# Key bits of the first head scaled on ScalarE, and one quarter of expert weights instead of two ahead of the first expert's tokens

## The chip, the cores and the metric

The kernel runs on one NeuronCore of one Trainium2 chip. Its engines work side by side, each through its own instructions in program order: PE (TensorE, matmuls; its weight loads are a row of their own, PEld), DVE (VectorE), ACT (ScalarE), POOL (GpSimd) and SP (SyncE, which here only issues DMAs). POOL also issues the DMAs that gather or scatter rows by an index. The metric is the device time of one execution in microseconds (us).

## The reference

Bucketed attention feeds a mixture of experts. Attention: a query and a key may meet only where the signs of six random projections agree.

```python
q_bits = (np.einsum('bhsd,dk->bhsk', q, proj) > 0)      # (4, 8, 768, 64) x (64, 6); k likewise
mask   = q_bucket[:, :, :, None] == k_bucket[:, :, None, :]
scores = np.where(mask, scale * np.matmul(q, k.transpose(0, 1, 3, 2)), -1e9)
attn   = softmax(scores); out = np.matmul(attn, v)
```

Mixture of experts on the 3072 rows of `out` (512 columns): tokens are assigned greedily, highest gate logit first, each of the 8 experts taking at most 384; then for each expert

```python
h = np.maximum(x[mask] @ w1[e], 0.0)     # w1: (8, 512, 1024)
out[mask] = h @ w2[e]                    # w2: (8, 1024, 512)
```

## The kernel before, in words

**Attention** takes the 32 heads in groups of four. Every float32 operand is split into a high and a low 16-bit half, so that products of halves replace one float32 product. The six sign bits of a query or key are six more rows of the stationary and moving operands `qa` and `ka`, scaled to plus or minus 4096 so that unequal buckets fall out of the softmax. `S_pass` (line 226) makes scores whose row maximum DVE takes (line 228), `m_rows` (line 241) writes that maximum back into `qa`, `ST` (lines 250 to 252) makes the scores again, transposed, with their exponential on ACT, and `AV` multiplies by the values.

**The opening** prepares the first group by hand, in the order written out in the string `OPS`: each word is a letter for a function and a number. `t0` (`top`) casts the first head's query and key, `b0` and `b1` (`tbits`) make the first head's query and key sign bits: PE projects (line 209), DVE compares and writes plus or minus 0.5 (line 210), and DVE multiplies by 8192 (line 211). `r0 r2 r1 r3` (`rest`, line 214) cast the halves for `qb` and `kb` on ACT, `c1 c0` (`cast`, line 123) those of heads 2 and 3, `l0 l1 l3 l2` (`rlo`, lines 216 and 217) and `u0 u1` (`sub`, line 126) subtract on POOL. `B0` and `D0` (`bits`, lines 134 to 140, and `bdma`, line 309) make the sign bits of the other three heads: PE projects, DVE compares into `bt` (line 139), DVE scales `bt` (line 140), and SP sends it off. The words `w2`, `w4`, `w5` are idle matmuls on `wrm` (line 72), whose result nobody reads.

**Routing** sorts tokens to experts in phases, one an expert; phase 0 decides who goes to expert 0, and so on. A phase is a chain of short steps that go between DVE (compare, line 496) and PE (count, lines 507 and 514). Phases 1 to 7 are run beside the previous expert's matmuls, at fixed steps of that work: phase 1 at the steps `E1`.

**The transition** (`start`) comes after phase 0 has found which rows of the weights and of the tokens expert 0 needs. `wload` has POOL gather weights (line 721): expert 0's first matrix in four quarters (128 x 1024 float32, 0.52 MB each), its second in two halves (1.05 MB each). `gather` has POOL fetch the 384 tokens in three pieces `xg` (line 713, 0.26 MB each). `wsplit` splits a quarter: ACT scales it into the high half `wh` (line 730) and the low half `wl` is made by DVE for the first two quarters (line 734), later by an ACT scaling (line 731) and a subtraction on POOL. `xsplit0` transposes a token piece on PE (line 766), ACT writes the high half `xh` (line 767) and DVE the low half `xl` (line 768); then come idle matmuls (`warm`, line 540), 7 after each piece, by `KW[6]`. `KW[5]` idle matmuls stand behind the last matmul of phase 0 (line 698), before the first piece.

**The experts** then run in steps of three matmuls of the first layer (line 780, 128x384 each, twelve to a block `f`, ACT's `hh` at line 782 after each block) or two of the second (line 792). The weights of expert 0's second matrix are split from step 2 on, ahead of the first `hh` in ACT's order.

The order on each engine is the order in which the Python code emits it (`manual_schedule`); waits are put in by the framework.

Of the kernel before, what the change touches and what calls it, by code (L numbers as in the profile page):

```python
# [14 lines left out]
ALU = mybir.AluOpType  # L15
# [27 lines left out]
def attention(tc, nc, ctx, qT, kT, vv, proj, wg, x_dram, L, jp, identf, B, late=None, after=None):  # L43
# [6 lines left out]
    V=nc.vector; A=nc.scalar; G_=nc.gpsimd; T=nc.tensor; SY=nc.sync  # L50
# [74 lines left out]
    def sub(G,w,p,eng=None):  # L125
        (eng or G_).tensor_tensor(TMP[G,'l'][w][:,p],LD[G][w][:,p],TMP[G,'h'][w][:,p],op=ALU.subtract)
# [78 lines left out]
    def tbits(w):  # L205
        dst=(QA,KA)[w][0][64:70,0,0:S]
        for hf in range(2):
            ps=psT.tile([128,512],F32,name="pst"); r=slice(hf*384,hf*384+384)
            T.matmul(ps[64:70,0:384],prt,(qd,kd)[w][0:64,0,r],start=True,stop=True,tile_position=(0,64))
            V.tensor_scalar(dst[:,r],ps[64:70,0:384],0.0,0.5,op0=ALU.is_gt,op1=ALU.subtract)  # L210
        V.tensor_scalar(dst,dst,8192.0,None,op0=ALU.mult)
    def rest(j,n):
        h=slice(64,128) if n<2 else slice(0,64); dst,src=((QB,qd),(KB,kd),(QB,qd))[n]
        A.copy(dst[0][h,j],src[h,j])
# [95 lines left out]
    def copies(a):  # L310
        for j in (0,2): SY.dma_start(a[1][64:128,j:j+2,0:S],a[0][64:128,2:4,0:S])
    OPS=dict(i=lambda j: init(j,A.copy),t=top,b=tbits,r=lambda n: rest(n//3,n%3),l=lambda n: rlo(n//2,n%2),
        c=lambda w: cast(0,w,1),u=lambda w: sub(0,w,1),s=lambda k: S_pass(k//6,k%6),B=lambda n: bits(0,[1]),D=lambda n: bdma(),
# [46 lines left out]
    for t in range(6*NH+LAG+6):  # L360
        h,s=divmod(t,6)
# [29 lines left out]
W2=[2,7,12,17]  # L391
XS=[56,56,57,57]
XD=[0,8,7,4]
KW=[1,0,4,0,2,19,7,1]
SC=16
XSC=8.0
WSC=64.0
class Moe:
# [143 lines left out]
    def phase(s,ph):  # L542
# [9 lines left out]
        if not last:  # L552
# [13 lines left out]
            for l,w in enumerate(WID):  # L566
# [3 lines left out]
                if l==0 or first:  # L570
# [3 lines left out]
                    if first:  # L574
                        if l==0: wp=s.wps(); s.warm(KW[7],wp)
                        s.warm(KW[0],wp)
                    for a,b in ((l+1,l+2),) if first else ((1,6),):
# [18 lines left out]
                T.matmul(n,s.us[l][0:J if first else 128],hit[0:J if first else 128],start=True,stop=True)  # L596
                if first: s.warm(KW[1],wp)
                elif l==0 and ph>1:
# [14 lines left out]
            T.matmul(pe[:,0:8],s.tiny,sat,start=False,stop=True)  # L613
            if first: s.warm(KW[2],wp)
            V.reduce_max(nn,pe[:,0:8],axis=AX.X)
# [24 lines left out]
        T.matmul(pp[:,0:2*NC],s.ones,cum,start=False,stop=True)  # L640
        if first: wp=s.psO.tile([128,512],F32,name="po"); s.warm(KW[3],wp)
        elif not last: s.fill()
# [32 lines left out]
        if first:  # L675
            pi=ps()
            for i,b in enumerate(blocks):
                members(*b)
                if not i: rr()
                collect(*b); s.warm(KW[4],wp)  # L680
        else:
# [76 lines left out]
    def xsplit0(s):  # L758

        xh,xl=s.W[0,'x']=(s.t([128,4,384],F16,"xh",bufs=1),s.t([128,4,384],F16,"xl",bufs=1))  # L760
        V=s.nc.vector; A=s.nc.scalar
        for c in range(3):
            px=(s.psX,s.psX,s.psA)[c].tile([128,512],F32,name=("px","px","psa")[c])
            r=slice(c*128,c*128+128); p4=px.rearrange("p (d q) -> p d q",d=4)
            for d in range(4):
                s.nc.tensor.transpose(p4[:,d],s.XG[0][:,c,d*128:d*128+128],s.identf)
            A.mul(xh[:,:,r],p4,XSC)  # L767
            V.scalar_tensor_tensor(xl[:,:,r],p4,XSC,xh[:,:,r],op0=ALU.mult,op1=ALU.subtract)
            s.warm(KW[6],s.wp)

    def layer1(s,ph,f,piece):
        T=s.nc.tensor
# [32 lines left out]
    def start(s):  # L805

        s.ps0=None; V=s.nc.vector
        s.wload(0,0,4,(0,1))
        next(s.ph0)
        s.gather(0)  # L810
        s.wload(0,0,4,(2,3))
        s.wsplit(0,0,0,V)
        next(s.ph0)
        s.ch=[s.phase(p) for p in range(8)]
        s.wsplit(0,0,1,V)
        s.wload(0,1,2)
        s.xsplit0()
        s.wsplit(0,0,2,by=14)
        s.wsplit(0,0,3,by=22)

# [86 lines left out]
```

## Time and profile before

| | us |
|---|---|
| three runs, median (lowest to highest) | 754.43 (754.01 to 759.91) |
| the profiled execution, its own time | 757.86 |
| its span, first to last instruction | 756.1 |
| PE busy in the span | 679.5 (90%) |
| DVE busy | 552.9 (73%) |
| ACT busy | 465.0 (61%) |
| POOL busy | 497.1 (66%) |

All durations below are from the one profiled execution, whose span is 756.1 us and which took 757.86 us in all, 3.43 us more than the median of the runs. "Idle before" in a row is the engine's own idle time ahead of that instruction, and the arrow names what ended it. The clock column of a table by stretch is TensorE's granted clock, 1.00 for 2.4 GHz and 0.50 for 1.2 GHz.

### The profile page before, as it was taken

To read this page: it belongs to the slowest core of one execution; us is meant where nothing else is said; L and a number is where in the kernel's file an instruction comes from. 1 tells how busy PE (TensorE), PEld (TensorE's weight loads), DVE (VectorE), ACT (ScalarE), POOL (GpSimd) and SP (SyncE) were. 2 spreads that over 40 slices of the span, in tenths; PEclk is the share of its full clock that TensorE was granted. 3 is DMA by queue.
4 is the path that set the end of the run, shared out by engine and by line. 5 is a ranking of instruction groups with operands and counts; after the bars stand their busy time and mean duration, and the time that the engine had idled before them with its cause. 6 is when DMAs were issued, how large, how long until landed. Compare 5 with 4: busy or idle time off the path is not lost. (4 is left out here: it accounts for less than half of the span.)

```text
span 756.1 us, 19028 instructions
## 1 busy us (share of the span) xinstructions
PE 679.5 (90%) x7789; PEld 438.1 (58%) x7789; DVE 552.9 (73%) x1178; ACT 465.0 (61%) x852; POOL 497.1 (66%) x436
## 2 busy tenths in 40 slices
PE   8898979999999999998988679999789899999995
PEld 2566656776767767666666454545445455555552
DVE  4979967888878888988985668676758878754120
ACT  6677666677776777665664063756547475756550
POOL 8587849697795977856664246474827382858671
PEclk9999999999999999999999589999999999999998
DMA  7638653625546255340001161616071717162611
GB/s 188 170 98 223 147 163 79 168 64 139 136 107 176 65 133 160 84 97 23 23 10 36 54 212 26 254 46 262 29 255 52 235 59 275 40 231 91 243 55 42
DMA packets 39951, 93.57 MB, mean 124 GB/s; under 512 B 4548, under 2 KB 30520, under 8 KB 37816
## 3 DMA queue, kind: packets, MB, share of 16 engines
q1 hardware_dynamic: 33048, 46.21, 23.5%
q0 software_dynamic: 6816, 46.15, 17.3%
q8 instruction: 61, 1.00, 0.6%
q14 instruction: 26, 0.21, 0.1%
HBM read 59.53 MB, written 12.58 MB: 95 GB/s over the span
## 5 line engine op out<-in xcount | busy, mean ns | idle before, releaser
L255 POOL TENSOR_TENSOR lo<-pt 128x768 f16<-128x768 f32 x143 | 233.8, 1646 | 78.3 <-ACT pt L252 64.8
L252 ACT ACTIVATE pt<-pst 128x384 f32<-128x384 f32 x384 | 182.9, 491 | 98.6 <-PE pst L251 85.6
L228 DVE TENSOR_REDUCE m<-pss 128x1 f16<-128x770 f32 x192 | 182.4, 955 | 38.2 <-PE pss L226 37.2
L250 PE MATMUL pst<-qa,ka 128*128 128x384 f16 x384 | 126.0, 328 | 6.7 <-DVE XT L294 3.6
L251 PE MATMUL pst<-qb,kb 128*128 128x384 f16 x384 | 125.9, 328 | 0.0
L267 PE MATMUL psv<-vh,lo 128*128 128x65 f16 x1152 | 121.6, 194 | 3.8 <-POOL lo L255 3.8
L265 PE MATMUL psv<-vh,pt 128*128 128x65 f16 x1152 | 121.8, 195 | 0.0
L266 PE MATMUL psv<-vl,pt 128*128 128x64 f16 x1152 | 121.8, 193 | 0.0
L265 PEld LDWEIGHTS <-pt 128*128 128x128 bf16 x1152 | 107.2, 98 | 13.0 <-issue 3.5
L266 PEld LDWEIGHTS <-pt 128*128 128x128 bf16 x1152 | 106.2, 99 | 9.8 <-issue 0.5
L267 PEld LDWEIGHTS <-lo 128*128 128x128 f16 x1152 | 106.2, 98 | 4.1 <-POOL lo L255 4.1
L226 PE MATMUL pss<-ka,qa 128*128 128x385 f16 x384 | 95.3, 330 | 14.1 <-DVE m L228 14.0
L730 ACT ACTIVATE wh<-wf 128x1024 f16<-128x1024 f32 x64 | 67.2, 1050 | 40.7 <-PE psa L698 21.1
L742 POOL TENSOR_TENSOR wl<-wf,wh 128x512 f16<-128x512 f32 x71 | 79.9, 1147 | 0.0
L780 PEld LDWEIGHTS <-wh 128*128 128x128 f16 x512 | 47.8, 97 | 39.3 <-issue 9.4
L731 ACT ACTIVATE wf<-wf 128x1024 f32<-128x1024 f32 x62 | 65.5, 1057 | 2.0
L783 DVE SCALAR_TENSOR_TENSOR hl<-px,hh 128x384 f16<-128x384 f32 x64 | 34.4, 551 | 41.2 <-ACT hh L782 40.8
L226 PEld LDWEIGHTS <-qa 128*128 128x128 f16 x384 | 37.5, 98 | 45.6 <-issue 23.2
L255 DVE TENSOR_TENSOR lo<-pt 128x768 f16<-128x768 f32 x49 | 61.0, 1246 | 1.5 <-ACT pt L252 1.0
L792 PEld LDWEIGHTS <-hh 128*128 128x128 f16 x384 | 36.5, 98 | 40.5 <-issue 2.5
L795 ACT ACTIVATE o<-po 128x512 f32<-128x512 f32 x24 | 14.2, 591 | 71.4 <-PE po L792 71.2
L780 PE MATMUL px<-xh,wh 128*128 128x384 f16 x256 | 53.2, 325 | 4.0 <-ACT xh L767 1.7
(253 smaller groups left out, 1328.1 us busy)
## 6 DMA issues: line engine op xcount, KB each, us to landing
vp<-in_vv_dram SPq DMA_DIRECT2D x8, 768.0 KB
x_dram<-X SPq DMA_DIRECT2D x16, 384.0 KB
qp<-in_qT_dram SPq DMA_DIRECT2D x7, 768.0 KB
kp<-in_kT_dram SPq DMA_DIRECT2D x7, 768.0 KB
qa<-qh SPq DMA_DIRECT2D x14, 192.0 KB
ka<-kh SPq DMA_DIRECT2D x14, 192.0 KB
qb<-qh SPq DMA_DIRECT2D x14, 192.0 KB
kb<-kh SPq DMA_DIRECT2D x14, 192.0 KB
```

The lines of the kernel that those rows point to most:

```text
L226: T.matmul(ps[:,hf,0:HK],QA[u][:,j,qc*128:qc*128+128],KA[u][:,j,hf*HK:hf*HK+HK],start=True,stop=True)
L228: V.tensor_reduce(M6[h][:,qc:qc+1],ps[:,:,0:HK],axis=AX.XY,op=ALU.max,negate=True)
L250: T.matmul(ps[:,0:384],KA[u][:,j,kr],QA[u][:,j,r],start=True,stop=False)
L251: T.matmul(ps[:,0:384],KB[u][:,j,kr],QB[u][:,j,r],start=False,stop=True)
L252: A.activation(PT[h,kc][0][:,r],ps[:,0:384],AF.Exp,scale=0.125)
L255: eng.tensor_tensor(l,p,p.bitcast(BF)[:,1::2],op=ALU.subtract)
L265: T.matmul(av[:,c,:],ph[:,r],VH[u][:,j,kc,:],start=(kc==0 and c==0),stop=False,skip_group_check=True)
L266: T.matmul(av[:,c,0:64],ph[:,r],VL[u][:,j,kc,:],start=False,stop=False,skip_group_check=True)
L267: T.matmul(av[:,c,:],l[:,r],VH[u][:,j,kc,:],start=False,stop=False,skip_group_check=True)
L730: s.nc.scalar.mul(h[:,r],f[:,r],WSC)
L742: for _ in range(n): s.nc.gpsimd.tensor_tensor(*s.pend.pop(0)[1],op=ALU.subtract)
L780: T.matmul(p[:,0:384],a[:,o:o+128],b[:,d],start=n==0,stop=n==11)
```

## The change

Four edits. In the opening, the scaling of the first head's key bits (`tbits(1)`, the word `b1`) goes from DVE to ACT; that of the query bits stays on DVE. In the transition, POOL gathers one quarter of the weights ahead of the tokens instead of two, and the split of the second quarter (`wsplit(0,0,1,V)`, one ACT and two DVE instructions) comes after the tokens' split instead of before it. The idle matmuls ahead of the first token piece go from 19 to 32. Those after the three pieces go from 7, 7, 7 to 6, 12, 7.

```diff
@@ tbits
-        V.tensor_scalar(dst,dst,8192.0,None,op0=ALU.mult)
+        if w: A.mul(dst,dst,8192.0)
+        else: V.tensor_scalar(dst,dst,8192.0,None,op0=ALU.mult)
@@
-KW=[1,0,4,0,2,19,7,1]
+KW=[1,0,4,0,2,32,(6,12,7),1]
@@ xsplit0
-            s.warm(KW[6],s.wp)
+            s.warm(KW[6][c],s.wp)
@@ start
-        s.wload(0,0,4,(0,1))
+        s.wload(0,0,4,(0,))
         next(s.ph0)
         s.gather(0)
-        s.wload(0,0,4,(2,3))
+        s.wload(0,0,4,(1,2,3))
         s.wsplit(0,0,0,V)
         next(s.ph0)
         s.ch=[s.phase(p) for p in range(8)]
-        s.wsplit(0,0,1,V)
         s.wload(0,1,2)
         s.xsplit0()
+        s.wsplit(0,0,1,V)
         s.wsplit(0,0,2,by=14)
         s.wsplit(0,0,3,by=22)
```

From line 211 on, a line of the kernel before has the next higher number in the changed one. **ACT in the opening**, from the first head's casts on (`qa`, `ka`: operands of the first head; `qb`, `kb`: their low parts' operands; `kh`, `qh`: halves of heads 2 and 3). Before:

```order
L204 CAST qa_167<-XT 64x768
L204 CAST ka_168<-XT 64x768
L214 CAST qb_169<-XT 64x768 x2
L214 CAST kb_170<-XT 64x768
L204 CAST qa_167<-XT 64x768
L204 CAST ka_168<-XT 64x768
L123 CAST kh<-kp 128x768
L123 CAST qh<-qp 128x768
```

Changed:

```order
L204 CAST qa_167<-XT 64x768
L204 CAST ka_168<-XT 64x768
L211 ACTIVATE ka_168<-ka_168 6x768
L215 CAST qb_169<-XT 64x768 x2
L215 CAST kb_170<-XT 64x768
L204 CAST qa_167<-XT 64x768
L204 CAST ka_168<-XT 64x768
L123 CAST kh<-kp 128x768
L123 CAST qh<-qp 128x768
```

The scaling stands third here, ahead of seven casts, and it reads what DVE wrote at line 210.

**ACT in the transition** (`wh_8728`: expert 0's first matrix, high half, a quarter to an instruction; the other `wh` and its `wf`: the second matrix). Before:

```order
L730 ACTIVATE wh_8728<-wf_8663 128x1024 x2
L767 ACTIVATE xh<-px 128x4x128 x2
L767 ACTIVATE xh<-psa 128x4x128
L730 ACTIVATE wh_8728<-wf_8663 128x1024
L731 ACTIVATE wf_8663<-wf_8663 128x1024
L730 ACTIVATE wh_8728<-wf_8663 128x1024
L731 ACTIVATE wf_8663<-wf_8663 128x1024
L730 ACTIVATE wh_8839<-wf_8764 128x1024
L731 ACTIVATE wf_8764<-wf_8764 128x1024
L782 ACTIVATE hh<-px 128x384
L582 ACTIVATE zE<-zD 128x24 x5
```

Changed:

```order
L731 ACTIVATE wh_8728<-wf_8663 128x1024
L768 ACTIVATE xh<-px 128x4x128 x2
L768 ACTIVATE xh<-psa 128x4x128
L731 ACTIVATE wh_8728<-wf_8663 128x1024 x2
L732 ACTIVATE wf_8663<-wf_8663 128x1024
L731 ACTIVATE wh_8728<-wf_8663 128x1024
L732 ACTIVATE wf_8663<-wf_8663 128x1024
L731 ACTIVATE wh_8856<-wf_8774 128x1024
L732 ACTIVATE wf_8774<-wf_8774 128x1024
L783 ACTIVATE hh<-px 128x384
L583 ACTIVATE zE<-zD 128x24 x5
```

The second quarter's instruction has moved from ahead of the three `xh` to behind them; all that follows is in the order it had.

**DVE in the transition** (`rem` to `nrem`: the end of phase 0; `zm`: the start of phase 1's decision). Before:

```order
L672 TENSOR_SCALAR nrem<-rem 128x8
L734 SCALAR_TENSOR_TENSOR wl_8729<-wf_8663,wh_8728 128x512 x2
L768 SCALAR_TENSOR_TENSOR xl<-px,xh 128x4x128 x2
L768 SCALAR_TENSOR_TENSOR xl<-psa,xh 128x4x128
L478 TENSOR_REDUCE zm<-Lm 128x24
```

Changed:

```order
L673 TENSOR_SCALAR nrem<-rem 128x8
L769 SCALAR_TENSOR_TENSOR xl<-px,xh 128x4x128 x2
L769 SCALAR_TENSOR_TENSOR xl<-psa,xh 128x4x128
L735 SCALAR_TENSOR_TENSOR wl_8729<-wf_8663,wh_8728 128x512 x2
L479 TENSOR_REDUCE zm<-Lm 128x24
```

The second quarter's low half now stands directly ahead of phase 1.

## Rows read from the trace of the kernel before

**Rows 1.** From the page: PE's busy share and its granted clock in 40 equal slices of the span, in tenths (9 is 90% or more).

```profile
PE   8898979999999999998988679999789899999995
...
PEclk9999999999999999999999589999999999999998
```

**Rows 2.** The timeline of the opening around the first head's bits, all engines: start, duration, engine, line, operation, and in brackets idle time before it and what ended it.

```profile
5.82 0.83 ACT L204 CAST ka<-XT 64x768 f16<-64x768 f32 x1
...
6.67 1.69 ACT L214 CAST qb<-XT 64x768 f16<-64x768 f32 x2
...
10.44 0.56 DVE L210 TENSOR_SCALAR ka<-pst 6x384 f16<-6x384 f32 x1 [0.20 <-PE pst L209]
...
11.03 0.45 DVE L211 TENSOR_SCALAR ka<-ka 6x768 f16<-6x768 f16 x1
...
12.87 0.15 PEld L226 LDWEIGHTS <-qa 128*128 128x128 f16 x1 [0.17 <-issue]
```

**Rows 3.** The same timeline, POOL's subtractions and a DVE instruction beside them.

```profile
7.92 1.64 POOL L217 TENSOR_TENSOR qb<-XT,qb 64x768 f16<-64x768 f32 x1
...
8.47 1.30 DVE L211 TENSOR_SCALAR qa<-qa 6x768 f16<-6x768 f16 x1
...
14.44 1.63 POOL L126 TENSOR_TENSOR kl<-kp,kh 128x768 f16<-128x768 f32 x1
```

**Rows 4.** Line 140, all eight of its instructions: durations in ns, shortest, median, longest.

```profile
L140 DVE TENSOR_SCALAR bt<-bt x8: 359/590/1654, 19.7 to 310.3; 128x768 f16<-128x768 f16 x8
```

**Rows 5.** The timeline behind the sign bits of the other heads, and the ends of the idle times of POOL and ACT there.

```profile
19.68 0.36 DVE L140 TENSOR_SCALAR bt<-bt 128x768 f16<-128x768 f16 x1
19.95 2.69 DVE L228 TENSOR_REDUCE m<-pss 128x1 f16<-128x770 f32 x3
...
20.96 0.49 PE L226 MATMUL pss<-ka,qa 128*128 128x385 f16 x2 [0.28 <-DVE m L228]
...
22.52 0.66 ACT L241 ACTIVATE qa<-pst,mbi,msc 32x384 f16<-32x384 f32 x1 [6.88 <-issue]
...
27.11 0.24 POOL L288 TENSOR_TENSOR wgs<-wgr,wgs 128x32 f16<-128x32 f32 x1 [9.32 <-issue]
```

**Rows 6.** POOL's timeline in the transition: weight quarters and halves (`wf`) and token pieces (`xg`). Other issues are left out.

```profile
428.93 1.14 POOL L721 DMA_INDIRECT wf<-in_w_dram,zwidx  x1 [20.55 <-DVE zmi L654]
...
432.71 0.95 POOL L713 DMA_INDIRECT xg<-x_dram,zidx  x1 [0.69 <-DVE zA L659]
...
436.65 0.98 POOL L721 DMA_INDIRECT wf<-in_w_dram,zwidx  x1 [0.30 <-issue]
```

**Rows 7.** PE's timeline from the end of phase 0 to the first layer.

```profile
433.17 2.19 PE L540 MATMUL po<-iot,mones 128*128 128x128 bf16 x19
436.81 1.12 PE L766 MATMUL px<-identf,xg 128*128 128x128 f32 x4 [1.45 <-DMA xg<-x_dram,zidx]
437.71 0.95 PE L540 MATMUL po<-iot,mones 128*128 128x128 bf16 x7
...
440.06 1.06 PE L766 MATMUL psa<-identf,xg 128*128 128x128 f32 x4
...
443.52 0.81 PE L780 MATMUL px<-xh,wh 128*128 128x384 f16 x4 [1.70 <-ACT xh L767]
```

**Rows 8.** ACT's timeline there and in the first steps of the first layer.

```profile
433.75 1.06 ACT L730 ACTIVATE wh<-wf 128x1024 f16<-128x1024 f32 x1 [21.08 <-PE psa L698]
435.87 1.06 ACT L730 ACTIVATE wh<-wf 128x1024 f16<-128x1024 f32 x1 [1.07 <-DMA wf<-in_w_dram,zwidx]
...
442.87 0.60 ACT L767 ACTIVATE xh<-psa 128x512 f16<-128x512 f32 x1 [2.71 <-remote]
...
447.44 1.04 ACT L730 ACTIVATE wh<-wf 128x1024 f16<-128x1024 f32 x1
...
449.85 0.66 ACT L582 ACTIVATE zE<-zD 128x24 bf16<-128x24 int32 x5
```

**Rows 9.** DVE and PE in the first steps of phase 1, from the timelines of both engines.

```profile
434.83 1.29 DVE L734 SCALAR_TENSOR_TENSOR wl<-wf,wh 128x512 f16<-128x512 f32 x2 [1.74 <-ACT wh L730]
...
444.11 0.34 DVE L478 TENSOR_REDUCE zm<-Lm 128x24 f32<-128x192 f32 x1
...
447.16 0.46 PE L507 MATMUL psa<-zOH,zcmp 128*128 128x8 bf16 x12 [0.55 <-DVE zcmp L496]
...
451.35 0.32 PE L514 MATMUL psa<-zOH,zcmp 128*128 128x32 bf16 x6 [0.84 <-DVE zcmp L496]
...
464.80 0.32 PE L514 MATMUL psa<-zOH,zcmp 128*128 128x32 bf16 x6 [0.83 <-DVE zcmp L496]
```

**Rows 10.** A table by stretch (start:end, length; busy us and instructions of PE, PEld, DVE, ACT, POOL; granted clock of PE; share of the DMA engines; GB/s). The first two stretches lie in attention, the others in the transition.

```profile
345.50:349.40 3.90, 1.96 (x39) 1.47 (x36) 3.83 (x6) 0.54 (x2) 2.40 (x2) 1.00 0.01 4
349.60:352.80 3.20, 3.00 (x15) 1.80 (x14) 2.22 (x5) 2.19 (x5) 1.47 (x1) 0.50 0.42 123
...
438.50:441.50 3.00, 3.00 (x23) 2.88 (x22) 1.38 (x2) 0.65 (x2) 2.39 (x3) 0.50 0.81 243
441.50:443.40 1.90, 0.32 (x4) 0.20 (x2) 0.00 (x0) 0.53 (x2) 0.20 (x1) 0.96 1.02 362
443.40:446.50 3.10, 2.98 (x18) 1.66 (x17) 2.97 (x12) 3.04 (x5) 0.00 (x0) 1.00 0.98 391
446.50:449.00 2.50, 1.53 (x30) 1.10 (x30) 2.06 (x9) 2.47 (x3) 0.00 (x0) 1.00 0.52 213
```

## The prediction

> **What bounds the kernel now.** Read the page first: PE is busy in nearly every slice, and its granted clock dips visibly in one place only, the 23rd and 24th slice, which are phase 0 and the transition [rows 1]. A microsecond lost ahead of PE's dense work is therefore lost at the end, and the change touches the two places where PE waits by design: the opening, up to 24 us, and the transition, from 428.9 to 451.4 us. I read each as a chain: who ends the wait of whom.
>
> In the opening, PE reaches the first scores at 12.87, through idle matmuls; the key bits are ready at 11.03 + 0.45 = 11.48 [rows 2], so line 211 binds nobody. The next thing that does is DVE: PE waits 0.28 at 20.96 for the first of three maxima, which follow line 140 on DVE without a gap [rows 5].
>
> In the transition PE ends its 19 idle matmuls and waits 1.45 for the first token piece, then works piece by piece at the low clock, and starts the first layer at 443.52 [rows 7]. What it gains there it can only keep if the next wait does not end later: PE stops again at 447.16 for phase 1's first compare and at 451.35 for the next one [rows 9]. These two waits end by other chains: DVE starts phase 1 at 444.11, and ACT makes `zE` at 449.85 at the end of a queue without a gap [rows 8, 9]. From 451.35 to the wait at 464.80 PE's timeline has no wait of note, so the time of the row at 451.35 is what the transition passes on to the end.
>
> **The scaling on ACT.** It removes 0.45 from DVE, which hides behind PE's idle matmuls: worth nothing. It adds one ACT instruction that cannot start before 10.44 + 0.56 = 11.00 and stands ahead of seven casts of which the first began at 6.67 [rows 2]. No row has this instruction on ACT; a cast of as many columns takes 0.83 (row at 5.82), DVE took 0.45, an ACT pass over 1024 columns 1.06 [rows 8]. I take 0.83 for the same column count, and 0.45 to 1.06 as bounds: done at 11.83, still 1.0 ahead of PE at 12.87. Without that cover it would cost its own excess over 0.45.
>
> The casts then run from 11.83 instead of 6.67, 5.16 later. ACT's own cover is the idle 6.88 before 22.52 [rows 5]: enough. POOL's first subtraction needs the first of the two casts: 11.83 + 1.69/2 = 12.7 instead of 7.92, so its unbroken row of six moves by 4.8. POOL's cover is the idle 9.32 before 27.11: enough too.
>
> But the move puts one of POOL's instructions beside line 140. The fifth, 14.44 to 16.07, goes to 19.2 to 20.9, and line 140 comes to its turn at 19.68. What that does is seen on DVE's instructions of this kind [rows 3, 4]: line 211 on the query bits began at 8.47 inside POOL's instruction of 7.92 to 9.56 and took 1.30, where the same on key bits took 0.45; line 140 itself takes between 0.36 and 1.65. If line 140 waits for POOL's end, it finishes at 20.9 + 0.2 = 21.05 instead of 20.04: the three maxima, PE's wait at 20.96 and all of PE behind it come 1.0 later. With 0.45 or 1.06 for the new instruction the same sum gives 0.65 or 1.25; if POOL's instruction misses line 140, nothing. I take 1.0.
>
> The Trainium skill, page "SBUF — State Buffer", section "SBUF: two separate sides", says that VectorE's fast modes and GpSimd share a port pair as an exclusive lock: who starts first keeps it for the whole instruction and the other blocks fully. By that rule the opening loses the 1.0; by the median of line 140 [rows 4], 0.59 against 0.36, it would lose 0.23.
>
> **The transition.** The token issues do not move: they wait for the indices at 432.71, not for the quarter ahead of them [rows 6]. The 13 more idle matmuls cost 13 x 0.103 (19 take 2.19, 7 take 0.95) = 1.34, so PE is free at 436.70 and finds the first piece landed, which before ended its wait at 436.81 with 0.52 MB more ahead of it. Between the first and the third piece stand 18 idle matmuls instead of 14. At the low clock the third piece comes at 440.06 - 0.11 + 4 x 0.107 = 440.4; if the clock rises as soon as the first piece is done, the 2.78 left between become 1.39 and it comes at 439.0. Transposes (1.06 or half) and `xh` (0.60) follow: first layer at 440.1 to 442.1, 1.4 to 3.4 earlier than 443.52. Of that, 1.75 is a stall: the third piece's transposes end at 441.12 by their row, but ACT starts only at 442.87, released by something that the profile does not name [rows 7, 8].
>
> Where the gain goes: into PE's next wait. The second quarter is issued in the slot of 436.65 to 437.63. The first took 433.75 - 430.07 = 3.68 from the end of its issue to ACT's start; the second so reaches ACT at 441.3. DVE starts its low half 1.08 behind ACT and needs 1.29 [rows 8, 9], so phase 1, now behind it, starts at 443.7 instead of 444.11, and PE's count comes at 446.7 instead of 447.16. PE, done with its 18 matmuls of 0.163 by 443.2 to 445.2, waits 1.5 to 3.5 there instead of 0.55.
>
> The row at 451.35 waits for ACT's queue, which now holds the second quarter behind `xh` (1.06 more) and then waits for loads that each come one place later. Behind the tokens must land three quarters and a half of the second matrix, 2.62 MB; before, DMA moved 0.73 + 0.69 + 1.21 = 2.63 MB from 438.5 to 446.5 [rows 10]. So the half of the second matrix lands at 446.5 by bytes. By the same count it was at 445.1 before, and ACT took it up at 447.44 at the latest: a lag of 0 to 2.3. I take 0.9, which gives 447.4: no change against 447.44, with 446.5 to 448.8 as bounds (-0.9 to +1.4).
>
> **Sum.** Against the profiled execution, 757.86: +1.0 and 0, 758.9. The median is 3.43 lower, and part of that may be the stall: in an execution without it ACT would have taken the half at 445.1 + 0.9 = 446.0, 1.4 earlier, and the changed order has nothing to gain from its absence. I count half, 0.7. So 754.43 + 1.0 + 0 + 0.7 = **756.1**, a slowdown of 0.2%. A measurement of this kernel can tell about 1%, 7.5 us, from no change.
>
> **Rivals.** *The tokens' lead survives* (faster). If the clock rises early, ACT has the third `xh` from 439.0 + 0.53 = 439.5, and then 0.60 and five passes of 1.06 to do, 5.9, before it wants the second matrix at 445.4. Behind the tokens 2.62 MB at 391 GB/s, the rate of 443.4 to 446.5 [rows 10], from 438.5 on are there at 445.2, with the lag at 445.2 to 446.1. ACT's first split of the second matrix then starts at 445.4 to 446.1 instead of 447.44; I take 445.9, and the row at 451.35 comes 1.5 earlier. Against it: DMA ran at 243 GB/s until 441.5, while no more loads were queued than will be now. The deciding point is that start: below 446.4 it outweighs the opening's 1.0. With the stall in the usual execution of before and the opening at 0 to 1.0 the time is 752.9 to 753.9; I take 753.4.
>
> *The clock falls in the longer wait* (slower). From 443.2 or 445.2 PE has little to do until 447, then twelve matmuls and another wait until 451.4. In attention the clock fell after 345.5 to 349.4, PE busy 1.96 of 3.90, and 349.6 to 352.8 ran at 0.50 [rows 10]. A fall of that kind around 450 doubles the time of every matmul for some 3.2 us of dense work, half of it lost, 1.6, on top of the forecast: 757.7. Against it: the two waits of before left the clock at 1.00 from 446.5 to 449.0.
>
> The Trainium skill, page "TensorE: Matmul & The Clock Gate", section "HAM oscillation — how this bites in real kernels", tells of a burst of matmuls shorter than the wait behind it, after which each burst starts slow. The new order makes that shape, 2.9 of matmuls and up to 3.5 of wait, and by that rule this rival's 757.7 would be the result.
>
> *The change does nothing*: line 140 misses POOL's instruction and the waits swallow the transition: 754.4.
>
> **How the numbers follow.** My forecast 756.1: 0.45, own range 754.9 to 757.5. The lead survives: 0.30. The clock falls: 0.15. Nothing: 0.08. The 0.02 left are disturbances that nothing here prices. The range takes in the rivals and the bounds of the sum (0 to 1.25, -0.9 to +1.4, 0 to 1.4): 752.6 to 759.4. No case reaches 7.5 us; for the scatter of the runs, whose highest was 759.91, I keep 0.03 on the slow side and 0.01 on the fast.
>
> **What would show it.** Line 140 first: about 1.3 long with POOL's subtraction beside it, and line 228 and the matmul of 20.96 one us later; 0.36 would refute the opening. Then no idle time ahead of the first transposes; the first layer's first matmul at 440 to 442; DVE's split of the second quarter just ahead of phase 1's first reduction; a wait of over 1.5 at the first count; ACT idle ahead of its second and third quarters; the second matrix's first split near 447.4. Wrong altogether would be a first split before 446, or a clock at 0.50 after 445.

## The result, and the profile after

The changed kernel is slower by about half a per cent: 758.91 us against 754.10 us as medians of 22 runs each, ratio 1.0056 (95% interval 1.0037 to 1.0075), which is 2.8 to 5.7 us. A second comparison, with the experiments, gave 1.0041 (1.0025 to 1.0057), 1.9 to 4.3 us. The forecast was 756.1 from 754.43, 1.7 us slower: the sign is right and the time lies in the whole range (752.6 to 759.4), but outside the 754.9 to 757.5 of the forecast itself, and the loss is two to three times as large in the first comparison (4.8 between the medians) and nearly twice in the second.

The profiled execution of the changed kernel took 755.75 us (span 754.0), less than that of the kernel before (757.86): attention, from ACT's first exponential to the first idle matmul behind phase 0, ran 6.9 us shorter in it, and the change touches nothing there. So spans are not compared here. Each stretch is measured from a mark of its own: the opening from the start of line 139 on DVE, the transition from the first idle matmul behind phase 0.

The page of the changed kernel, PE's busy share and granted clock in 40 slices; the one dip, at the 22nd to 24th slice, answers to the one in [rows 1].

```profile
PE   8898898999999999998997679899889999999995
...
PEclk9999999999999999999998589999999999999998
```

**The opening.** The timeline of the changed kernel, to hold against [rows 2, 3, 5]. Columns as there; line numbers are one higher from line 211 on.

```profile
8.64 0.35 DVE L212 TENSOR_SCALAR qa<-qa 6x768 f16<-6x768 f16 x1
...
11.20 0.84 ACT L211 ACTIVATE ka<-ka 6x768 f16<-6x768 f16 x1 [4.56 <-DVE ka L210]
11.95 1.67 ACT L215 CAST qb<-XT 64x768 f16<-64x768 f32 x2
...
18.90 0.96 DVE L139 TENSOR_SCALAR bt<-pss 128x768 f16<-128x768 f32 x1 [2.14 <-PE pss L138]
19.31 1.63 POOL L126 TENSOR_TENSOR kl<-kp,kh 128x768 f16<-128x768 f32 x1
19.90 1.27 DVE L140 TENSOR_SCALAR bt<-bt 128x768 f16<-128x768 f16 x1
...
22.09 0.49 PE L227 MATMUL pss<-ka,qa 128*128 128x385 f16 x2 [1.20 <-DVE m L229]
```

The scaling took 0.84 on ACT and hid, the casts went 5.3 later, POOL's `kl` came to lie on line 140, and line 140 lasted 1.27 until just after POOL's end (20.94) instead of 0.36. PE's wait grew from 0.28 to 1.20.

**The transition.** PE, then ACT, in the changed kernel, to hold against [rows 7, 8].

```profile
427.42 3.58 PE L541 MATMUL po<-iot,mones 128*128 128x128 bf16 x32
430.79 1.03 PE L767 MATMUL px<-identf,xg 128*128 128x128 f32 x4
...
431.99 0.64 PE L767 MATMUL px<-identf,xg 128*128 128x128 f32 x4
...
433.27 0.63 PE L767 MATMUL psa<-identf,xg 128*128 128x128 f32 x4
433.74 0.56 PE L541 MATMUL po<-iot,mones 128*128 128x128 bf16 x7
439.31 1.44 PE L781 MATMUL px<-xh,wh 128*128 128x384 f16 x4 [5.02 <-ACT xh L768]
...
448.08 0.32 PE L515 MATMUL psa<-zOH,zcmp 128*128 128x32 bf16 x6 [0.23 <-DVE zcmp L497]
```

```profile
432.79 0.60 ACT L768 ACTIVATE xh<-px 128x512 f16<-128x512 f32 x1 [3.65 <-PE px L767]
437.12 0.60 ACT L768 ACTIVATE xh<-px 128x512 f16<-128x512 f32 x1 [3.73 <-remote]
438.66 0.60 ACT L768 ACTIVATE xh<-psa 128x512 f16<-128x512 f32 x1 [0.95 <-remote]
...
444.18 1.04 ACT L731 ACTIVATE wh<-wf 128x1024 f16<-128x1024 f32 x1
```

PE finds the first piece landed, as forecast, and its three transposes end by 433.90. But ACT starts on the second and third piece only at 437.12 and 438.66, released by "remote", a word that names no engine of this core and that stood once in the profile before, at the third piece [rows 8]. I call these the late signals. The first layer starts 11.88 after the first idle matmul; before it was 10.35. In this wait the clock falls: 6.70 us at 1.00, then 6.60 at 0.50.

```profile
431.70:438.40 6.70, 2.59 (x34) 2.37 (x33) 1.34 (x2) 1.19 (x2) 4.02 (x5) 1.00 0.93 293
438.60:445.20 6.60, 5.89 (x24) 2.78 (x24) 5.62 (x15) 6.48 (x7) 0.00 (x0) 0.50 0.68 283
```

The row on which the transition was to be judged, the first matmul of line 514 (515), comes 448.08 - 427.42 = 20.66 after the first idle matmul; before 451.35 - 433.17 = 18.18 [rows 7, 9]. Opening and transition of this pair of profiles lose 0.9 + 2.5. In both profiles ACT took up the second matrix without a wait, so this 2.5 is ACT's queue: it has the third piece 1.5 later after the first idle matmul (11.24, before 9.70), and the second quarter's split, 1.0, now stands behind it.

### The profile page after: what moved, and what is told of

It reads as the page before. It is cut to its first block, busy times and chain, and to the rows that moved or that the text cites. A ratio compares the mean times of both kernels' runs of the same rounds, so it can differ in the third digit from the quotient of the medians.

```text
span 754.0 us, 19061 instructions
## 1 busy us (share of the span) xinstructions
PE 680.7 (90%) x7806; PEld 438.5 (58%) x7806; DVE 547.9 (73%) x1177; ACT 464.8 (62%) x853; POOL 496.7 (66%) x436
## 5 line engine op out<-in xcount | busy, mean ns | idle before, releaser
L781 PEld LDWEIGHTS <-wh 128*128 128x128 f16 x512 | 48.7, 99 | 45.5 <-issue 16.5
L781 PE MATMUL px<-xh,wh 128*128 128x384 f16 x256 | 55.4, 336 | 7.1 <-ACT xh L768 5.0
L256 DVE TENSOR_TENSOR lo<-pt 128x768 f16<-128x768 f32 x49 | 59.1, 1206 | 1.5 <-ACT pt L253 1.0
```

The costliest lines, as they stand in the source:

```text
L256: eng.tensor_tensor(l,p,p.bitcast(BF)[:,1::2],op=ALU.subtract)
L781: T.matmul(p[:,0:384],a[:,o:o+128],b[:,d],start=n==0,stop=n==11)
```

## The experiments

All twelve transitions are in one table, with the two profiles from before the experiments; each number is counted from the first idle matmul behind phase 0 in that run's trace, from unrounded times; the last column is the end of that matmul. "Half" is ACT's first split of the second matrix, with ACT's own wait for that load in brackets (none: its queue was full).

| kernel | first layer | half | first 514 | last matmul of expert 0 |
|---|---|---|---|---|
| before | 10.35 | 14.27 (none) | 18.18 | 50.20 |
| before again | 8.71 | 14.24 (1.08) | 18.15 | 51.49 |
| opening only | 8.78 | 13.93 (1.13) | 17.84 | 51.17 |
| opening, POOL later | 9.06 | 14.06 (0.98) | 17.98 | 51.33 |
| opening, line 140 on ACT | 8.94 | 14.56 (1.59) | 18.47 | 51.79 |
| idle matmuls only | 7.58 | 14.29 (0.35) | 18.20 | 51.53 |
| all but the load order | 7.39 | 14.69 (1.87) | 18.61 | 50.63 |
| changed | 11.88 | 16.76 (none) | 20.66 | 52.69 |
| changed again | 7.35 | 15.36 (0.49) | 19.28 | 51.31 |
| transition only | 7.33 | 15.71 (1.42) | 19.63 | 51.67 |
| load and split order only | 7.91 | 16.69 (2.22) | 20.61 | 53.95 |
| changed, late second matrix | 7.32 | behind `zE` | 18.74 | 50.89 |
| before, late second matrix | 8.78 | behind `zE` | 15.81 | 47.85 |
| the same, with idle matmuls | 7.61 | behind `zE` | 15.80 | 48.64 |

In the first eleven rows line 514 follows the half by 3.90 to 3.92, whatever the first layer did. In these rows that is the chain: half, its second pass, `hh`, `zE`, DVE's compare.

**Opening only.** The kernel before with `A.mul` for the key bits.

```diff
-        V.tensor_scalar(dst,dst,8192.0,None,op0=ALU.mult)
+        if w: A.mul(dst,dst,8192.0)
+        else: V.tensor_scalar(dst,dst,8192.0,None,op0=ALU.mult)
```

> The kernel before with the first edit alone: ACT scales the first head's key bits. Theory A (the opening's delay reaches the end, because PE has no later wait in attention that takes it up): line 140 lasts about 1.27 beside POOL's subtraction, ACT's first exponential comes about 1.1 later (24.9 for 23.7), and the whole takes 0.9 to 1.3 longer than before, a ratio near 1.0015. Rival B (the delay is taken up by a later wait and the change's loss is all of the transition): the first exponential is 1.1 later but the time is within 0.3 of before.

Measured: 1.0015 (0.9987 to 1.0044), which separates neither theory. What both start from did not come, since line 140 took only 0.55. (The 23.7 and 24.9 in this text and in a later one are the starts of PE's first matmul of `ST`; ACT's first exponential stands at 24.26 before and 25.39 in the changed kernel, the same 1.1 apart.)

```profile
17.61 1.65 POOL L126 TENSOR_TENSOR ql<-qp,qh 128x768 f16<-128x768 f32 x1
17.93 0.96 DVE L139 TENSOR_SCALAR bt<-pss 128x768 f16<-128x768 f32 x1 [2.29 <-PE pss L138]
18.92 0.55 DVE L140 TENSOR_SCALAR bt<-bt 128x768 f16<-128x768 f16 x1
19.21 1.76 POOL L126 TENSOR_TENSOR kl<-kp,kh 128x768 f16<-128x768 f32 x1
```

Here PE's projections, and so line 139, came about 1 us earlier than in the changed kernel's profile, and line 140 began inside the subtraction ahead of `kl`, 0.34 before that one's end (17.61 + 1.65 = 19.26). It ended 0.21 after it, just as line 140 of the changed kernel ended 0.23 after `kl`. So it did not miss POOL; it met an instruction that was nearly over.

From the start of line 139 to ACT's first double exponential it takes 5.77, against 5.57 or 5.58 in seven profiles with the old opening (an eighth, the kernel before again, is told with that run). Where line 140 began inside `kl`, it was 6.49 (changed), 6.68 (changed again, line 140 lasting 1.47) and 6.78 (changed with late second matrix, 1.57). So the opening costs 0.9 to 1.2 or 0.2, by how much of a subtraction of POOL is left when line 140 begins.

**Transition only.** The changed kernel with DVE's scaling back.

```diff
-        if w: A.mul(dst,dst,8192.0)
-        else: V.tensor_scalar(dst,dst,8192.0,None,op0=ALU.mult)
+        V.tensor_scalar(dst,dst,8192.0,None,op0=ALU.mult)
```

> The changed kernel without the first edit: order of loads, place of the second split, and idle matmuls as in the changed kernel. Theory A: from the first idle matmul behind phase 0 to phase 1's first decision matmul (18.2 before, 20.7 in the changed kernel) it takes 20.2 to 21.2, the first layer starts 11.5 to 12.2 after that idle matmul (10.4 before), and the time is 2 to 3.5 above before, a ratio of 1.003 to 1.0045. Rival B (the late signal of the token transposes was one execution's accident, and the changed kernel loses elsewhere): that stretch is within 0.7 of 18.2 and the time within 1 of before.

Measured: 1.0007 (0.9975 to 1.0038). Both theories are half wrong. The late signals are gone and the first layer starts at 7.33, yet line 514 is at 19.63: later than 18.2 without them. ACT waits for the half of the second matrix.

```profile
438.28 1.06 ACT L730 ACTIVATE wh<-wf 128x1024 f16<-128x1024 f32 x1 [1.45 <-DMA wf<-in_w_dram,zwidx]
439.67 1.06 ACT L730 ACTIVATE wh<-wf 128x1024 f16<-128x1024 f32 x1 [0.33 <-DMA wf<-in_w_dram,zwidx]
445.26 1.06 ACT L730 ACTIVATE wh<-wf 128x1024 f16<-128x1024 f32 x1 [1.42 <-DMA wf<-in_w_dram,zwidx]
```

**Load and split order only**, idle matmuls and opening as before.

```diff
-KW=[1,0,4,0,2,32,(6,12,7),1]
+KW=[1,0,4,0,2,19,(7,7,7),1]
```

> Of the transition's edits the order of loads and splits alone, idle matmuls 19 and 7, 7, 7 as before, opening as before. Theory A1 (the order makes PE's signals for the second and third token piece late, since all of POOL's issues and the weights' transfers follow the tokens at once): the first layer starts over 11 after the first idle matmul, the stretch of 18.2 takes over 20, time 2 to 3.5 above before. Theory A2 (the idle matmuls do it, by holding PE or by moving the clock's rise ahead of the wait): the first layer starts under 9.5 after the first idle matmul, the stretch is within 1 of 18.2 and the time within 1 of before.

Measured: 1.0019 (0.9988 to 1.0051). Line 514 is at 20.61, as the order's theory has it, but with no late signal (first layer 7.91): the mechanism in that theory is wrong, its place right. Of the other theory only the first layer came true. The half waits 2.22 for its load, at 16.69.

**Idle matmuls only**, in the kernel before.

```diff
-KW=[1,0,4,0,2,19,7,1]
+KW=[1,0,4,0,2,32,(6,12,7),1]
```

> Of the transition's edits the idle matmuls alone (32 and 6, 12, 7), order of loads and splits and the opening as before. Theory A1 (the order does it): the first layer starts 10.4 to 10.9 after the first idle matmul, the stretch of 18.2 within 0.7, time within 1 of before. Theory A2 (the idle matmuls do it): late signals of 3 to 5 for the second and third piece here too, first layer over 11.5, time 2 to 3.5 above before.

Measured: 0.9999 (0.9966 to 1.0033). The first layer starts at 7.58, better than either theory had it, and line 514 at 18.20 all the same. A lead of 1.2 over the old idle matmuls (8.8) is worth nothing at the next mark: the half is at 14.29.

From here on theory C: the load order makes the second matrix's first half land later, and ACT's `hh` and `zE` are queued behind that wait.

**The changed kernel with a late second matrix.** ACT's first split of the second matrix goes behind the first `zE`.

```diff
-            for q in range(4): add(NS*k+W2[q],s.wsplit,k,1,q,None,NS*k+BY[2] if k<6 else 0)
+            for q in range(4): add(NS*k+(W2[q] if k else (7,9,12,17)[q]),s.wsplit,k,1,q,None,NS*k+BY[2] if k<6 else 0)
```

> The changed kernel, with ACT's first split of expert 0's second matrix moved behind its first zE (steps 7 and 9 for 2 and 7 of the first two quarters). Theory C (what the transition's edits cost is the later landing of the second matrix's first half, 13.9 after the first idle matmul with the old order of loads and 15.7 to 16.7 with the new, and ACT's hh and zE are queued behind that wait): zE no longer waits for it, the first matmul of line 515 comes 16.5 to 17.7 after the first idle matmul instead of 19.6 to 20.7 (18.5 if the token signals are late again), and the time falls to within 1.2 of before plus the opening's 1.1. Rival D (the loss is PE's longer wait for phase 1's compare and the clock's fall there): the stretch stays at 19.5 or more and the time at 2.5 to 4 over before.

Measured: 0.9998 (0.9974 to 1.0023), and line 514 at 18.74. No loss against before is left to measure, but the mark misses the 16.5 to 17.7 forecast. The loads are late all the same: ACT waits 1.32 for the second quarter of the first matrix and 2.44 for the third. DVE begins phase 1 behind the second quarter's split, so PE's first count comes at 13.94, and behind that wait PE's matmuls run slowly (granted clock 0.56 on average from 445.10 to 448.40). PE reaches line 515 only at 448.24, when DVE's compare has been ready since 447.17 + 0.56 = 447.73. That is rival D's mechanism, the longer wait at the first count and the clock's fall there; it shows once the half is out of the way.

```profile
441.59 1.06 ACT L731 ACTIVATE wh<-wf 128x1024 f16<-128x1024 f32 x1 [2.44 <-DMA wf<-in_w_dram,zwidx]
443.44 0.46 PE L508 MATMUL psa<-zOH,zcmp 128*128 128x8 bf16 x12 [3.53 <-DVE zcmp L497]
445.25 1.49 PE L781 MATMUL px<-xl,wh 128*128 128x384 f16 x4
447.17 0.56 DVE L497 TENSOR_TENSOR zcmp<-zd,tb 128x768 bf16<-128x768 bf16 x1
448.24 0.30 PE L515 MATMUL psa<-zOH,zcmp 128*128 128x32 bf16 x6
```

**The kernel before with a late second matrix**, the same line of diff.

> The kernel before with the same move of ACT's first splits of the second matrix. Theory C: line 514 comes 15.3 to 16.5 after the first idle matmul instead of 17.9 to 18.2, and as much of these 1.7 to 2.7 as no later wait takes is gained, so 0.5 to 2.5 less time than before. Rival D: the stretch is 17.5 or more, time within 0.5 of before.

Measured: 750.26 us, ratio 0.9960 (0.9937 to 0.9983): faster than both kernels, and by more in the median (4.1) than theory C's 0.5 to 2.5. ACT goes from `hh` to `zE` almost without a gap and line 514 comes at 15.81, with no wait of PE ahead of it.

```profile
440.06 0.47 ACT L782 ACTIVATE hh<-px 128x384 f16<-128x384 f32 x1
440.70 0.67 ACT L582 ACTIVATE zE<-zD 128x24 bf16<-128x24 int32 x5 [0.17 <-DVE zD L491]
441.28 1.06 ACT L730 ACTIVATE wh<-wf 128x1024 f16<-128x1024 f32 x1
```

Expert 0 ends 3.3 to 3.9 earlier than in the five old transitions without a late signal (51.17 to 51.79): 2.0 to 2.7 of it by line 514, the rest because the clock does not fall behind it (below).

So the late second matrix does not undo the change; it helps both kernels. With it in both, the changed kernel still takes 754.74 against 750.26, 4.5 more between the medians of twelve runs each (3.7 between the means). In this pair of profiles the marks come near the time: expert 0 ends 50.89 - 47.85 = 3.0 later, and the opening takes 6.78 - 5.57 = 1.2 longer.

**The opening with line 140 on ACT**, the opening's edit and this one.

```diff
-        V.tensor_scalar(bt[r],bt[r],8192.0,None,op0=ALU.mult)
+        if G==0: A.mul(bt[r],bt[r],8192.0)
+        else: V.tensor_scalar(bt[r],bt[r],8192.0,None,op0=ALU.mult)
```

> The opening's edit alone, and line 140 of the first group on ACT too, so that DVE has no fast instruction of one operand beside POOL's subtraction. Theory A (line 140 is held for as long as POOL's instruction runs, and that alone makes the 1.1): the first of the three maxima starts at 19.7 to 20.0 (21.1 in the changed kernel, 19.95 before) and the first exponential at 23.4 to 23.8 (24.9 and 23.7), time within 0.5 of before. Rival (POOL's later subtractions slow DVE's maxima or ACT as well): the first exponential still at 24.3 or later.

Measured: 0.9985 (0.9958 to 1.0012). DVE's maxima go on at once (19.27), but the exponential comes 5.98 after line 139, 0.4 later than before and not earlier. ACT's cover, idle 6.88 before [rows 5], is used up by the casts that came 5.3 later and this instruction: its queue reaches `m_rows` without a gap.

```profile
21.82 0.93 ACT L187 CAST vh<-vp 128x384 f16<-128x384 f32 x2
22.67 1.64 POOL L126 TENSOR_TENSOR kl<-kp,kh 128x768 f16<-128x768 f32 x1
22.77 0.66 ACT L243 ACTIVATE qa<-pst,mbi,msc 32x384 f16<-32x384 f32 x1
```

**All but the load order.** The changed transition with two quarters ahead of the tokens again, opening as before.

```diff
-        s.wload(0,0,4,(0,))
+        s.wload(0,0,4,(0,1))
         next(s.ph0)
         s.gather(0)
-        s.wload(0,0,4,(1,2,3))
+        s.wload(0,0,4,(2,3))
```

> Two quarters of the weights ahead of the tokens as before, opening as before, but the second quarter's split behind the tokens' and idle matmuls 32 and 6, 12, 7 as in the changed kernel: of the transition's edits all but the order of loads. Theory C (the order of loads makes the second matrix late): its first half is split 13.8 to 14.4 after the first idle matmul, line 514 comes at 17.8 to 18.3, time within 0.7 of before. Rival E (the place of the split makes the loss, since phase 1 begins on DVE behind it): line 514 at 19.3 or later.

Measured: 1.0004 (0.9981 to 1.0027). Line 514 at 18.61 and the half at 14.69, 0.3 over the upper ends forecast and 0.7 under the lowest of the new load order. ACT waits 1.87 for the half, so the load is still what it waits for. The half is 0.1 to 0.8 later than with the split in its old place (13.93 to 14.56), and that is all that the moved split can have cost here. Against the transition alone, which differs from this run in the order of loads only, the half comes 1.0 earlier (14.69, 15.71).

**Late second matrix and idle matmuls together**, in the kernel before.

> The kernel before with ACT's first splits of the second matrix behind zE and with the changed kernel's idle matmuls (32 and 6, 12, 7). Theory C (without the queue on ACT, PE's next wait is phase 1's compare, which follows the tokens' split on DVE, so that a lead of the tokens is now worth something): first layer at 7.4 to 7.7 after the first idle matmul, phase 1's first count at 11.1 to 11.5 instead of 12.4, line 514 at 14.3 to 15.0 instead of 15.8, and 3 to 5 less time than before. Rival F (another wait takes it, as it did with the idle matmuls alone): line 514 at 15.5 or later, time as with the move alone, 2 to 4 less than before.

Measured: 0.9969 (0.9944 to 0.9994). First layer at 7.61 and first count at 11.25 as theory C had it, but line 514 at 15.80, not earlier: theory C misses and rival F holds. Another load ends the chain, the fourth quarter:

```profile
441.01 1.06 ACT L730 ACTIVATE wh<-wf 128x1024 f16<-128x1024 f32 x1 [1.38 <-DMA wf<-in_w_dram,zwidx]
442.10 1.06 ACT L731 ACTIVATE wf<-wf 128x1024 f32<-128x1024 f32 x1
443.06 0.47 ACT L782 ACTIVATE hh<-px 128x384 f16<-128x384 f32 x1
```

**The changed kernel again**, and **the kernel before again**, unaltered.

> The changed kernel once more. Theory A (PE's late signals for the token pieces are an event of single executions and not of this order): ACT takes the second and third piece within 0.1 of the end of their transposes, the first layer starts 7.3 to 7.6 after the first idle matmul and line 515 still comes at 19.3 to 20.7, since the second matrix's landing sets it. Rival G (the order brings them): the signals are late by over 3 again, first layer at 11.5 to 12.2. Time 1.002 to 1.007 of before in either case.

> The kernel before once more. Theory A: the third piece's signal is not late, the first layer starts 8.6 to 9.0 after the first idle matmul instead of 10.35, and line 514 comes 17.7 to 18.3 after it all the same. Rival G: it is late by over 1.5 again.

Measured: 1.0041 (1.0025 to 1.0057) and 0.9985 (0.9960 to 1.0010), the latter a measure of what such an interval is worth. Neither profile shows a late signal; first layer at 7.35 and 8.71, line 514 at 19.28 and 18.15, as theory A had it (19.28 just under its 19.3).

The profiled execution of the kernel before took 761.62, the longest of its nine; the next took 754.46. Its opening shows why, and it is the very instruction that the change moves: line 211 on the key bits lasted 4.94 us on DVE, where it takes 0.35 to 0.47 in the other seven profiles with the old opening. It began at 11.24, with POOL's second subtraction for `kb`, and ended 0.22 after the third subtraction from there (14.33 + 1.63 = 15.96). In the other seven it began 0.08 to 0.22 ahead of that second subtraction.

```profile
11.24 4.94 DVE L211 TENSOR_SCALAR ka<-ka 6x768 f16<-6x768 f16 x1
14.33 1.63 POOL L126 TENSOR_TENSOR kl<-kp,kh 128x768 f16<-128x768 f32 x1
16.32 0.80 PE L226 MATMUL pss<-ka,qa 128*128 128x385 f16 x2 [2.72 <-DVE ka L211]
```

PE waited 2.72 for it and then worked slowly (0.85 for two matmuls of 128x385 as late as 25.61, where it takes 0.49 from 15.05 on in the first profile), and ACT's first exponential came at 32.00 instead of 23.4 to 24.6. Moved to ACT, the same scaling took 0.84 in the profiles with the new opening. How often the long case happens no run shows; it stood in one profile of eight, and it is too rare to move the medians: the other eight executions of that run lie between 750.50 and 754.46.

The loads, in equal stretches of 4 us from the first idle matmul (the last two columns are the share of the DMA engines and GB/s), first the changed kernel, then the kernel before:

```profile
429.65:433.65 4.00, 4.00 (x36) 4.00 (x36) 2.06 (x8) 1.06 (x1) 3.09 (x4) 0.50 0.47 131
433.65:437.65 4.00, 3.71 (x40) 3.23 (x40) 2.29 (x5) 1.79 (x3) 3.08 (x4) 0.88 0.82 237
437.65:441.65 4.00, 2.44 (x15) 1.27 (x13) 2.60 (x9) 2.33 (x3) 1.33 (x2) 1.00 0.98 331
```

```profile
436.76:440.76 4.00, 2.48 (x22) 2.21 (x22) 2.16 (x9) 2.04 (x2) 3.09 (x4) 0.50 0.77 246
440.76:444.76 4.00, 4.00 (x28) 3.81 (x27) 2.78 (x6) 1.27 (x3) 3.08 (x4) 0.50 0.77 210
444.76:448.76 4.00, 3.67 (x26) 2.12 (x23) 3.27 (x12) 3.59 (x4) 0.70 (x1) 0.97 0.96 305
```

In the first stretch the new order moves 4.00 x (246 - 131) = 460 KB less, nearly the quarter (0.52 MB) that used to be issued while routing still computed the tokens' indices. POOL stands idle for 2.68 just ahead of that stretch, waiting for the indices, where it waited 0.69 [rows 6].

```profile
429.20 0.98 POOL L714 DMA_INDIRECT xg<-x_dram,zidx  x1 [2.68 <-DVE zA L660]
```

What is not sent there is sent later, ahead of the half that ACT wants. Two things then make the half late, and no run separates them: these bytes, on DMA engines that are 0.96 to 0.98 busy in the third stretch, and the half's own issue on POOL, one slot later (437.11 - 429.65 = 7.46 after the first idle matmul, before 443.28 - 436.76 = 6.52).

The same two runs show where the clock falls. In the changed kernel the stretch at 0.50 lies ahead of PE's wait for line 515 (at 448.93); in the kernel before it comes behind its wait for line 514 (at 454.92):

```profile
444.90:448.20 3.30, 3.30 (x12) 1.29 (x10) 0.63 (x2) 3.16 (x9) 0.00 (x0) 0.50 0.25 107
448.30:451.60 3.30, 2.67 (x23) 1.70 (x24) 2.36 (x9) 3.27 (x5) 2.42 (x3) 1.00 0.00 0
```

```profile
451.80:455.20 3.40, 0.94 (x12) 0.46 (x10) 1.27 (x3) 3.34 (x10) 0.27 (x2) 1.00 0.08 34
455.30:458.60 3.30, 3.30 (x13) 1.60 (x12) 1.81 (x8) 2.70 (x5) 2.05 (x2) 0.50 0.00 0
```

From line 514 to expert 0's last matmul it takes 32.02 to 32.04 in the first case and 33.32 to 33.35 in the second (the difference of the last two columns of the table): the same fall costs nothing or 1.31. (Of the rows with a late second matrix, not counted here, two lie between, at 32.15 and 32.84.) The old load order pays it in five of seven transitions; the changed one did not pay it in its own two nor in the transition alone.

**The opening with POOL's subtractions later**, the opening's edit and this one in the string `OPS`.

```diff
-... u0 u1 s7 v1 l2 ...
+... s7 v1 l2 u0 u1 ...
```

> The opening's edit alone, with POOL's subtractions for heads 2 and 3 put behind the one that waits for a late cast, so that POOL does nothing beside line 140. Theory A (POOL's instruction, if it began first, holds line 140 until it ends): line 140 lasts 0.36 to 0.40 and ACT's first double exponential starts 5.5 to 5.7 after line 139 starts, as before (5.58), instead of 5.8 to 6.8. Rival: 6.2 or more, so that something else in the moved row of casts holds the opening.

Measured: 0.9990 (0.9969 to 1.0010). Line 140 is back at 0.36, and the exponential comes 24.75 - 19.17 = 5.58 after line 139, as before. POOL was not quite idle: its subtraction for `qb` had ended 0.02 before line 140 began (18.50 + 1.65 = 20.15), its `ql` began 0.06 after it, and it was `ql` that got longer.

```profile
20.17 0.36 DVE L140 TENSOR_SCALAR bt<-bt 128x768 f16<-128x768 f16 x1
20.23 1.80 POOL L126 TENSOR_TENSOR ql<-qp,qh 128x768 f16<-128x768 f32 x1
```

## Why the prediction was right, and where not

**The scaling on ACT: right.** 0.84 against 0.83, hidden; casts 5.3 later against 5.16; line 140 at 1.27 against about 1.3; the loss 0.91 in that profile, 1.1 and 1.2 in two more, against 1.0. In the opening alone it was 0.2, under the 0.65 to 1.25 of the sum: `kl` missed line 140, but the subtraction ahead of it did not. The Trainium skill's rule of the shared port (page "SBUF — State Buffer", section "SBUF: two separate sides") agrees with these rows: line 140 ended 0.21 to 0.23 after the subtraction in which it began, whether 0.34 or 1.04 to 1.34 of it was left.

One term of this part was too small in one execution. The 0.45 that the edit removes from DVE, "worth nothing", was 4.94 in the second profile of the kernel before, and PE waited 2.72 for it. The prediction had seen that POOL can hold this instruction (1.30 on the query bits) and had not asked it of the key bits.

**The token issues do not move, PE finds the first piece landed, the first layer starts 1.4 to 3.4 earlier: right in a usual execution.** The changed kernel started it at 7.35, 1.4 ahead of 8.71 and 3.0 ahead of 10.35. Its first profile showed the opposite, 11.88, by the late signals.

**The gain goes into PE's next wait: right.** The changed kernel waits 3.22 at the first count in its second profile (1.5 to 3.5 was the forecast; 2.65 to 3.67 in the three other profiles of the new order without late signals). The idle matmuls alone show it best: 1.1 to 2.8 earlier at the first layer, nothing at line 514.

**ACT's first split of the second matrix "no change", 0 with bounds -0.9 to +1.4: this is the step that failed.** It came at 15.36 to 16.76 after the first idle matmul instead of 13.93 to 14.56, and line 514 with it: 1.1 later in the second pair, inside the bounds, and 2.5 in the first, where the late pieces held ACT's queue. The byte count was good: 446.5 against 445.1, 1.4 later, and 1.0 (15.71 against 14.69) and 1.1 (15.36 against 14.24) were measured. The term that was mis-sized is the lag from the landing by bytes to ACT, taken at 0.9 out of 0 to 2.3. In the kernel before without the stall ACT took the half at 14.24, which is 433.17 + 14.24 = 447.4 in the profile that the prediction read: a lag of 2.3. With it the new order comes at 446.5 + 2.3 = 448.8, the upper bound, +1.4.

Behind this lies a reading. The 447.44 of [rows 8] has no wait in it: ACT had been held up by the late third piece and came to the load late itself, so the row couldn't tell whether the load had long been there. In four profiles of the old transition without that delay ACT waited 0.98 to 1.59 for the half, and 0.35 with the idle matmuls: the landing sets it, and a later landing passes on.

**Half of the stall counted as part of the median, +0.7: wrong in kind.** With the stall line 514 came at 18.18, without it at 18.15. The stall hid in the same wait for the half, so it explains none of the 3.43 between the profiled execution and the median. It is the same lag again: without the stall the half was expected at 446.0, and it came at 447.4. That the forecast of +1.7 came as near as it did to the second comparison's 1.9 to 4.3 is in part luck: the 0.7 that was counted for the stall stood in for most of the 1.1 that was left out for the half.

**The rival "the clock falls in the longer wait", 0.15 and +1.6, was half right.** The clock falls: 438.60 to 445.20 in the first profile of the changed kernel (11.2 to 17.8 after the first idle matmul) and 444.90 to 448.20 in the second (15.3 to 18.6). Counted from the first idle matmul before, 433.17, that is at 0.50 after 445, which the prediction had named as a sign of being wrong altogether. But in the second profile, without late signals, it falls ahead of a wait that goes on until 448.93, where it is free, while the kernel before usually pays 1.31 for a fall behind its own wait. So this rival had the fall right and its price, 1.6, wrong. The Trainium skill (page "TensorE: Matmul & The Clock Gate", section "HAM oscillation — how this bites in real kernels") says that a burst shorter than the wait behind it is followed by a burst that starts slow; the trace shows the slow start, and that its price here depended on what PE waited for next. "The lead survives" fell with the half: no new order had it before 15.36.

**What stays open.** Opening and the end of expert 0 together lose 0.9 + 2.5 in the first pair of profiles, near the 2.8 to 5.7 measured. In the second pair expert 0 ends 0.2 earlier in the changed kernel, and its opening takes 1.1 more than the usual one of before (that of the second profile before lost more, by line 211): 0.9 together, less than the 1.9 to 4.3. That profiled execution took 753.59, the lowest of its twelve runs, 1.5 under their median, and what the others lost no trace shows. Neither part has a loss of its own clear of the noise: 1.0015 (0.9987 to 1.0044) for the opening, 1.0007 (0.9975 to 1.0038) for the transition. Two things that cost the new order more were each seen once: the late signals (52.69) and a second fall of the clock (53.95 in the load and split order alone). Whether they make the rest was not settled. Nor was the cause of the late signals: they stood in the first profile of either kernel and in none of the twelve later ones, two of these with the same orders of instructions, so the order alone does not make them.

## What to carry to other kernels

Before costing a load that is moved, ask in the trace whether the consumer waited for it; a row without a wait behind a queue that was itself late says nothing about when the load landed. In the transition this change sent 0.5 MB after an index-bound gather instead of in the gap while the index was computed, which put line 514 back by 1.0 to 2.5, though the transition alone shows no loss in time clear of the noise. What helped, in both kernels, was not on the loads at all but on ACT: whatever the critical chain needs (`hh`, `zE`) should not be queued behind a wait for data that is wanted later, worth 0.4% here (0.9960 in the kernel before). And an instruction that moves an engine's whole queue by 5 us may be free on that engine and still collide with a third one. Last, look at the slowest execution too: a term that is 0.4 us in seven profiles was 4.9 in the eighth.

## What the runs showed of the hardware

- A scaling on DVE (0.36 us for 128x768 f16) that began inside one of POOL's subtractions (1.63 to 1.65 us) ended 0.21 to 0.23 after that subtraction: 0.55 with 0.34 of it left, 1.27 to 1.57 with 1.04 to 1.34 left. Begun 0.06 ahead of a subtraction, and 0.02 behind the one before, it took 0.36, and POOL's took 1.80. And once a scaling (6x768), begun at the same hundredth as a subtraction, was held through three subtractions in a row, 4.94 us; begun 0.08 to 0.22 ahead of that subtraction it took 0.35 to 0.47 in seven profiles.
- ACT took up finished transposes up to 4.8 us after the end of PE's rows (433.27 + 0.63 = 433.90 by the row, 438.66 on ACT), with no engine named. It did not recur in twelve profiles. The cause is not known.
- The same stretch of PE at the low clock cost 1.31 us behind a wait and nothing ahead of one that went on for longer (448.93 in the changed kernel again); where PE got to line 515 after the compare was ready, it cost part of that (448.24 against 447.73).
